# A gated Fourier and expert-mixing kernel: sums of the hidden DFT begun earlier with two raw buffers, gate products stored a piece later, z loaded ahead, row transposes spaced anew

## The chip, the core and the metric

The kernel runs on one core of one Trainium2 chip. The time is device microseconds (us) of one execution. TensorE is called PE, VectorE DVE, ScalarE ACT, GpSimd POOL, and the queue that issues most loads SP. The kernel before was timed three times: 816.06, 817.18 and 818.11 us; the median is 817.18 us. The profile is one further execution of the same program, which took 815.7 us.

## The reference

With x of 2048 rows (the sequence) by 640 columns (hidden), cut to what is computed:

```
a = x @ dft_hid_re.T;  b = x @ dft_hid_im.T
y = dft_seq_re @ a - dft_seq_im @ b               # Fourier part
q = x @ w_q  -> 32 heads, two halves of 128
s1 = q1 @ k1.T;  s2 = q2 @ k2.T                    # 16 scores each
best two of s1, best two of s2, best two of their sums -> expert numbers, softmax g
out = sum over heads and picks of g * gelu(x . u[expert]) * v[expert]    # 256 experts
result = sig * y + (1 - sig) * out,   sig = sigmoid(sum(x * gate_w))
```

Every fp32 product is made of three matmuls (`mm3`, lines 123 to 127): each operand is split into a rounded high part and a low rest, and high-high, high-low and low-high are added up in PSUM.

## The kernel before

**Pieces.** The sequence DFT comes first and runs for most of the span. Two matrices (real, imaginary) by 4 column blocks of 512 give 8 *quarters* q of 16 *pieces* n each, 128 pieces in all. `seq_piece(n)` (line 193) starts the load of piece n+5 on SP, splits piece n+3 (high part on ACT, low part on POOL, `split_piece`, line 160), and multiplies x, kept in SBUF as the tiles X0 to X15, with piece n: 5 banks by 3 matmuls, 15 matmuls of 512 columns. The five products stay in banks 0 to 4 for a quarter. At a quarter's last piece ACT copies them into the five staging slots ST. Then `load_row` (line 180) loads the gate row, `gate_piece` (line 184) multiplies the five slots by it on DVE and issues each one's store to the DRAM scratch P (`pd`) on the ACT queue, right behind its multiply. For the first quarter the row is loaded at piece 18 and multiplied at piece 19; for the later ones the row is loaded at the quarter's last piece and multiplied at the second piece of the next quarter.

**What runs beside the pieces.** `at(n, f)` hangs a function on piece n, and `follow(n)` runs these after the piece's matmuls. A `Pump` (line 41) hands out other work in portions: after every `mm3` it gets a credit of 0.68 us times a share, and takes portions from its queues while it has credit. A function that puts much work on DVE draws credit off. The Pump also has a list `apart` of functions that come a given time after one another (`space`, `tick`): the transposes of the expert rows (`row_tile` in `rows`, line 458) are put there, the first with 12 us (20 us in the last group), the others with 4 us. `tick` adds to `clock` whether the list is empty or not.

In the first quarters the weights of the query are folded with the keys (`w_part`, `w_transposes`, lines 284 and 299), then the scores, the picks on DVE (`topk`, `gates`) and the row transposes follow. After the last row transpose the pool `p3` opens (in the loop, line 865), and `experts(g)` (line 512) begins for two groups of 16 *chunks*: for each chunk DVE builds two one-hot tiles `pt` and `qt` (lines 528 to 530), PE makes 16 small matmuls (line 550) into bank 5 or 6 in turn, in the last part always into bank 7, and DVE sums them into `cd` (lines 535 and 537). One chunk's tiles are built ahead of the matmuls of the one before.

**The last part.** The hidden DFT is made as a block product with sums and differences, 2 halves b by 35 *steps* m. The units of 5 steps each are a11, a12, s1, s2, s4, s3, a22. In the last quarter the sums of the DFT matrix D are made: `load_dt` (line 597) loads two rows of blocks into one raw tile, `make_sums` (line 610) makes five sums on DVE into one tile `tf`, `split_sums` (line 623) splits them on ACT, POOL and DVE into tiles that lie over the parts of x that are no longer needed. `load_v` and `split_v` do the same for v. Each step splits the operand of the step five later (`split_step`, line 684). The operands are loaded from P by SP into raw tiles that `take` hands out, `add_a` adds the ones that are sums. `load_z` loads the gate row, the activations and the expert sums gd for one block of 512 columns, `split_z` multiplies them and splits the result into `zo`, and `z_group` multiplies `zo` with v at the end of a12, of s4 and elsewhere. `load_z` first drains the Pump until the experts of its half are summed. It stands at steps 3 and 21 of each half, `split_z` four steps later.

All engines run their own instructions in program order. A waiting instruction holds up all that stands behind it on its engine or queue.

Of the kernel before, what the change touches and what calls it, by code (L numbers as in the profile page):

```python
# [8 lines left out]
F32 = mybir.dt.float32  # L9
F32R = mybir.dt.float32r  # L10
# [6 lines left out]
P = 128  # L17
S = 2048
D = 640
# [5 lines left out]
NT = S // P  # L25
NP = NT // 2
TC = 512
NC = S // TC
NPC = 2 * NC * NT
KD = D // P  # L30
# [10 lines left out]
class Pump:  # L41
# [8 lines left out]
        self.clock = 0.0  # L50

    def space(self, f, us):
        self.apart.append((f, us))

    def tick(self, us):
# [33 lines left out]
def gated_mix_kernel(ctx: ExitStack, tc: tile.TileContext, xT, xn, dreT, dimT, wsre, wsim, wq, kT, uT, vv, gw, out):  # L89
    nc = tc.nc  # L90
# [3 lines left out]
    big = ctx.enter_context(tc.tile_pool(name="big", bufs=1))  # L94
# [9 lines left out]
    def bank(n, shape=(P, TC), dt=F32):  # L104
        return psum.tile(list(shape), dt, name=f"b{n}", tag=f"b{n}")
# [4 lines left out]
    def ps_t(shape, dt=F32):  # L110
        return bank(7, shape, dt)
# [3 lines left out]
    def stage():  # L115
        return ST[:, rotate("st", 5)]

    def split(f, h, l, eng):

        nc.scalar.activation(h, f, AF.Copy)  # L120
        eng.tensor_sub(l, f, h.bitcast(F32))  # L121

    def mm3(o, wh, wl, ah, al, first, last, more=False):

        nc.tensor.matmul(o, wh, ah, start=first, stop=False, skip_group_check=more)  # L125
        nc.tensor.matmul(o, wh, al, start=False, stop=False, skip_group_check=more)  # L126
        nc.tensor.matmul(o, wl, ah, start=False, stop=last, skip_group_check=more)  # L127

    pd = dram.tile([2, NC, KD, P, TC], F32, name="pd")
# [3 lines left out]
    bg = Pump()  # L133

    def run_bg(us):
        bg.run(us, 0.95 if p3 is None else 0.9 if last_part else 1.0)


    WU = big.tile([P, 2 * KD * (HH * E + NE)], F32R, name="WU", tag="WU")
# [10 lines left out]
    pf, psp, X, xr = {}, {}, {}, {}  # L150

    def load_piece(n):
        if n < NPC:
            w, c, s = pieces[n]
            pf[n] = big.tile([P, TC], F32, name="wf", tag="wf", bufs=5)
            nc.sync.dma_start(pf[n], (wsre, wsim)[w][c, s])
# [3 lines left out]
    def split_piece(n):  # L160
        if n < NPC:
            psp[n] = WS[:, n % 4, 0], WS[:, n % 4, 1]
            split(pf.pop(n), *psp[n], nc.gpsimd)
# [4 lines left out]
    def at(n, f, *args):  # L168
        then.setdefault(n, []).append(lambda: f(*args))

    def follow(n):
        for f in then.pop(n, ()):
            f()


    banks = []
    p3, last_part = None, False
    grow, staged = {}, {}

    def load_row(q):  # L180
# [3 lines left out]
    def gate_piece(q):  # L184
        g = grow.pop(q)
        w, c = divmod(q, NC)
        for d in range(KD):
            f = staged.pop((q, d))
            nc.vector.scalar_tensor_tensor(f, f, -1.0 if w else 1.0, g, op0=OP.mult, op1=OP.mult)
            bg.credit -= 0.75  # L190
            nc.scalar.dma_start(pd[w, c, d], f)

    def seq_piece(n):
        w, c, s = pieces[n]
        if s == 0:
            banks[:] = [bank(d) for d in range(KD)]
        load_piece(n + 5)
        split_piece(n + 3)
        h, l = psp.pop(n)
        for d in range(KD):  # L200
            ds = slice(d * P, (d + 1) * P)
            mm3(banks[d], X[s][:, 0, ds], X[s][:, 1, ds], h, l, s == 0, s == NT - 1)
            if s == NT - 1:
                staged[n // NT, d] = f = stage()
                nc.scalar.activation(f, banks[d], AF.Copy)
            run_bg(0.68)

    for q in range(2 * NC):
        n = NT * (q + 1)
        at(n + (2 if q == 0 else -1), load_row, q)  # L210
        at(n + (3 if q == 0 else 1), gate_piece, q)


    p1_stack = ctx.enter_context(ExitStack())
# [32 lines left out]
    t = ps_t([P, 512])  # L247
# [70 lines left out]
    xf, xs = {}, {}  # L318
# [19 lines left out]
    n = 3  # L338
    for m in range(0, NWQ, 2):
        n = 4 + m if m < 14 else 17 + (m - 14) * 10 // 16  # L340
# [37 lines left out]
    picked, rowed = set(), set()  # L378
# [121 lines left out]
    for p in range(NP):  # L500
        n = N0 + 5 * p
# [4 lines left out]
    N1 = N0 + 5 * NP  # L506
# [88 lines left out]
    TS, T = {}, {}  # L595

    def load_dt(k):
        T["f"] = big.tile([P, 2, D], F32, name="dt", tag="xf")
        for w in range(2):
            nc.sync.dma_start(T["f"][:, w], (dreT, dimT)[w][k])  # L600

    def t_sum(k, n, a):

        if n < 2:
            return TS[k][:, (2 * n + a) * 2 * P:][:, :2 * P]
        if n == 2:
            return TS[5 + k // 2][:, (2 * (k % 2) + a) * 2 * P:][:, :2 * P]
        return DD[:, 0, a, k, 2 * P:4 * P] if n == 3 else TS[k][:, PAIR + a * P:][:, :P]

    def make_sums(k):  # L610
        if k == 0:
            T["t"] = big.tile([P, 9 * P], F32, name="tf", tag="xl")
        f, t = T["f"], T["t"]
        b11, b12, b21, b22 = (f[:, n, a * 2 * P:(a + 1) * 2 * P] for n in range(2) for a in range(2))
        t1, t5, t3, t6 = (t[:, n * 2 * P:(n + 1) * 2 * P] for n in range(4))
        nc.vector.tensor_sub(t[:, :4 * P].rearrange("p (n d) -> p n d", n=2), f[:, :, 0:2 * P], f[:, :, 2 * P:4 * P])
        nc.vector.scalar_tensor_tensor(t3, t1, -1.0, b22, op0=OP.mult, op1=OP.subtract)
        nc.vector.tensor_sub(t5, t1, t5)
        nc.vector.tensor_sub(t6, b22, b12)
        nc.vector.tensor_sub(t[:, 8 * P:], f[:, 1, 4 * P:], f[:, 0, 4 * P:])  # L620
        bg.credit -= 3.0

    def split_sums(k):
        for n in [k] + ([5 + k // 2] if k % 2 == 0 else []):
            TS[n] = big.tile([P, 2 * D], F32R, name="ts", tag=f"X{n}")
        t = T["t"]
        t1, t5, t3, t6 = (t[:, n * 2 * P:(n + 1) * 2 * P] for n in range(4))
        for n, f in enumerate((t1, t3, t5, t6, t[:, 8 * P:])):
            split(f, t_sum(k, n, 0), t_sum(k, n, 1), nc.gpsimd if n < 3 else nc.vector)
        bg.credit -= 1.0  # L630

    def load_v():
# [12 lines left out]
        return TS[5 + a][:, PAIR:].rearrange("p (k d) -> p k d", k=2)  # L645

    for k in range(KD):
        at(NPC - 13 + 2 * k, load_dt, k)
        at(NPC - 11 + 2 * k, make_sums, k)
        at(NPC - 10 + 2 * k, split_sums, k)  # L650
    at(NPC - 2, load_v)
    at(NPC - 1, split_v)


    raw_free, raw_tags = deque(), [("wf", 1)] * 5 + [(f"X{s}", 2) for s in range(10, 16)] + [("xf", 2)]
# [28 lines left out]
    def split_step(m):  # L684
        if m < 2 * NSTEP:
            b, (u, k) = m // NSTEP, divmod(m % NSTEP, KD)
            what = UNITS[u]
            key = (b, "s" if what in ("s1", "s2", "s4") else what, k)
            sp[m] = ring(m)[:, 0], ring(m)[:, 1]
            split(raw[key], *sp[m], nc.vector if what in ("s2", "s3") else nc.gpsimd)  # L690
            bg.credit -= 0.8 if what in ("s2", "s3") else 0.0
            if what in ("a11", "a12", "a22", "s3", "s4"):
                give(key)
# [148 lines left out]
    for b in range(2):  # L842
        M = NPC + b * NSTEP
        for k in range(KD):
            at(M - (8 if b else 6) + k, load_a, b, "a11", k, 1, 1)
            at(M - (4 if b else 2) + k, load_a, b, "a12", k, 1, 2)
            at(M + k, load_a, b, "s", k, 2, 2)
            at(M + k, load_a, b, "s3", k, 2, 1)
            at(M + 4 + k, add_a, b, "s", "s3", k, False)
            at(M + 5 + k, load_a, b, "a11", k, 1, 1)  # L850
            at(M + 8 + k, add_a, b, "s", "a11", k, False)
            at(M + 8 + k, add_a, b, "s3", "a11", k, True)
            at(M + 10 + k, load_a, b, "a12", k, 1, 2)
            at(M + 13 + k, add_a, b, "s", "a12", k, True)
            at(M + 21 + k, load_a, b, "a22", k, 2, 2)
        for n, i in ((0, 3), (1, 21)):
            at(M + i, load_z, b, n)
            at(M + i + 4, split_z, b, n)

    prep_split = {NPC - 4: (0,), NPC - 3: (1,), NPC - 2: (2,), NPC - 1: (3, 4)}  # L860
    WP = None
    for n in range(N0, NPC):
        seq_piece(n)
        follow(n)
        if n >= N1 and p3 is None and len(rowed) == NT and n % NT not in (0, NT - 1):
            p2_stack.close()
            p3 = ctx.enter_context(tc.tile_pool(name="p3", bufs=1, reuse_waits="tile"))
            pools.append(p3)
            WP = p3.tile([P, 2, 2, TC], F32R, name="WP")
            for g in range(2):  # L870
                bg.add(experts(g), late=True)
        for m in prep_split.get(n, ()):
            split_step(m)
    assert p3 is not None

    last_part = True
# [49 lines left out]
```

## Time and profile before

| what | value |
|---|---|
| median of three runs | 817.18 us |
| the profiled execution | 815.7 us |
| its span, first to last instruction | 813.7 us |
| PE busy | 789.6 us (97%) |
| DVE busy | 539.5 us (66%) |
| POOL busy | 340.9 us (42%) |
| ACT busy | 271.8 us (33%) |
| mean granted PE clock | 0.987 |

Matmuls overlap, so PE's busy time says only that some matmul was under way. In the timeline each row has the start, the duration, the engine, the line and the operation with its tiles. A bracket gives the time that the engine stood idle before it and what released it. In the table by stretches each engine's busy time is followed by its number of instructions; the clock is that which the throttle granted to PE (1.00 is full).

### The profile page before, as it was taken

The numbers are of one execution on the slowest core, as the hardware profiler recorded it, in microseconds if no ns is written. First come the engines' busy times: TensorE is split into PE (matmuls) and PEld (weight loads), VectorE is DVE, ScalarE is ACT, GpSimd is POOL, SyncE is SP. The second block draws the span as 40 slices with busy tenths as digits, with TensorE's granted clock in tenths as the row PEclk, the third lists the DMA queues.
The fourth block names the chain that finished last, engine by engine and source line by source line (L and its number), as shares of the span: only waits on it lengthen the run. The fifth ranks groups of instructions, "written<-read, shape, count | busy, mean of one in ns | idle before, by whom it ended". The sixth has DMA issues, their size and how long they took to land.

```text
span 813.7 us, 10931 instructions
## 1 busy us (share of the span) xinstructions
PE 789.6 (97%) x4167; PEld 627.9 (77%) x4167; DVE 539.5 (66%) x652; ACT 271.8 (33%) x444; POOL 340.9 (42%) x239
## 2 busy tenths in 40 slices
PE   8999899999999999999998999999999897999997
PEld 6677567888888888888886777777778675888886
DVE  4851201376887799689878397767768899637651
ACT  3434124322317134322613721311313442434350
POOL 5433133415334142342414674333336664567370
PEclk9999999999999999999999999999999998999999
DMA  9876984603023230214213533234333597397521
GB/s 344 304 280 185 321 317 130 212 1 110 14 98 102 86 110 14 97 48 139 99 41 114 166 120 92 91 117 130 95 119 117 176 294 235 91 296 235 178 94 64
DMA packets 62643, 119.55 MB, mean 147 GB/s; under 512 B 8832, under 2 KB 15616, under 8 KB 62336
## 3 DMA queue, kind: packets, MB, share of 16 engines
q1 hardware_dynamic: 49984, 101.55, 37.6%
q10 hardware_dynamic: 12608, 17.31, 5.9%
q8 instruction: 32, 0.52, 0.3%
q14 instruction: 19, 0.16, 0.1%
HBM read 98.91 MB, written 19.93 MB: 146 GB/s over the span
## 4 chain that ended last, share of the span: by engine, by line
PE 82%; DMA 6%; DVE 6%; ACT 2%; issue 2%; SPq 1%; POOL 1%; ACTq 0%; DVEq 0%; POOLq 0%
PE b L125 26%; PE b L127 25%; PE b L126 25%; PE b L291 2%; DMA ra<-pd 1%; DMA xr<-in_xn 1%; PE b L550 1%; DMA grow<-gdr 1%; DMA wf<-in_wsre 1%; ACT rows L467 1%; PE b L303 1%; DMA wf<-in_wsim 1%; DMA pd<-ST 1%; POOL WS L121 0%; DVE pt L530 0%
## 5 line engine op out<-in xcount | busy, mean ns | idle before, releaser
L121 POOL TENSOR_TENSOR WS<-wf,WS 128x512 fp32r<-128x512 f32 x128 | 186.8, 1465 | 297.1 <-ACT WS L120 295.6
L125 PE MATMUL b<-WS,X 128*128 128x512 f32 x640 | 257.1, 402 | 1.2 <-ACT X L120 1.2
L127 PE MATMUL b<-WS,X 128*128 128x512 f32 x640 | 250.6, 392 | 0.7 <-DVE X L121 0.6
L126 PE MATMUL b<-WS,X 128*128 128x512 f32 x640 | 250.6, 392 | 0.6 <-POOL WS L121 0.6
L125 PEld LDWEIGHTS b<-WS,X 128*128 128x128 f32 x640 | 120.5, 188 | 34.9 <-issue 7.9
L127 PEld LDWEIGHTS b<-WS,X 128*128 128x128 f32 x640 | 120.6, 188 | 27.6 <-DVE X L121 1.5
L126 PEld LDWEIGHTS b<-WS,X 128*128 128x128 f32 x640 | 120.7, 189 | 24.2 <-POOL WS L121 1.0
L120 ACT ACTIVATE WS<-wf 128x512 fp32r<-128x512 f32 x128 | 80.9, 634 | 139.1 <-PE b L127 85.6
L405 DVE TENSOR_REDUCE mm<-sc 128x64 f32<-128x1024 f32 x32 | 39.0, 1219 | 49.8 <-ACT sc L391 49.2
L121 POOL TENSOR_TENSOR xl<-xf,xh 128x640 fp32r<-128x640 f32 x16 | 32.6, 2059 | 73.5 <-ACT xh L120 73.5
L391 ACT ACTIVATE sc<-b 128x512 f32<-128x512 f32 x32 | 20.7, 647 | 127.2 <-PE b L127 114.5
L125 PE MATMUL b<-WU,xh 128*128 128x512 f32 x160 | 62.5, 391 | 0.0
L126 PE MATMUL b<-WU,xh 128*128 128x512 f32 x160 | 62.3, 389 | 0.0
L127 PE MATMUL b<-WU,xl 128*128 128x512 f32 x160 | 62.3, 389 | 0.0
L121 POOL TENSOR_TENSOR WS<-ra,WS 128x512 fp32r<-128x512 f32 x32 | 47.1, 1490 | 30.1 <-ACT WS L120 30.1
L535 DVE TENSOR_TENSOR tmp<-b,mask 128x512 f32<-128x512 f32 x32 | 22.0, 689 | 39.0 <-PE b L550 39.0
L306 DVE TENSOR_TENSOR WU<-b,WU 128x512 fp32r<-128x512 f32 (+1 forms) x16 | 7.8, 490 | 60.0 <-ACT WU L305 60.0
L407 DVE TENSOR_TENSOR eq<-sc,mm 128x1024 f16<-128x1024 f32 x32 | 46.3, 1446 | 1.1
L529 DVE TENSOR_TENSOR qt<-rows,wtab 128x1024 f16<-128x1024 f16 x32 | 32.8, 1025 | 14.3 <-PE b L466 14.3
L411 DVE TENSOR_REDUCE rr<-eq 128x64 f16<-128x1024 f16 x32 | 39.0, 1220 | 1.1
L467 ACT ACTIVATE rows<-b 128x384 f16<-128x384 f16 x16 | 30.7, 1916 | 26.6 <-PE b L466 26.6
L120 ACT ACTIVATE WS<-ra 128x512 fp32r<-128x512 f32 x46 | 28.1, 628 | 33.3 <-PE b L127 10.6
(145 smaller groups left out, 1256.7 us busy)
## 6 DMA issues: line engine op xcount, KB each, us to landing
wq<-in_wq SPq DMA_DIRECT2D x32, 640.0 KB, 6.3
ra<-pd SPq DMA_DIRECT2D x70, 256.0 KB, 4.6
wf<-in_wsre SPq DMA_DIRECT2D x64, 256.0 KB, 5.5
wf<-in_wsim SPq DMA_DIRECT2D x64, 256.0 KB, 2.7
pd<-ST ACTq DMA_DIRECT2D x40, 256.0 KB, 2.3
xr<-in_xn SPq DMA_DIRECT2D x16, 320.0 KB, 6.2
xf<-in_xT SPq DMA_DIRECT2D x16, 320.0 KB, 3.3
out_y<-ST ACTq DMA_DIRECT2D x7, 512.0 KB, 3.4
```

Source lines behind the costliest of these rows:

```text
L120: nc.scalar.activation(h, f, AF.Copy)
L121: eng.tensor_sub(l, f, h.bitcast(F32))
L125: nc.tensor.matmul(o, wh, ah, start=first, stop=False, skip_group_check=more)
L126: nc.tensor.matmul(o, wh, al, start=False, stop=False, skip_group_check=more)
L127: nc.tensor.matmul(o, wl, ah, start=False, stop=last, skip_group_check=more)
L391: nc.scalar.activation(scs[i].rearrange("p h e -> p (h e)")[:, c], ps, AF.Copy)
L405: nc.vector.tensor_reduce(m, sc, op=OP.max, axis=AX.X)
L407: nc.vector.tensor_tensor(eq, sc, m[:, :, None].to_broadcast([P, HH, E]), op=OP.is_equal)
L411: nc.vector.tensor_reduce(r, eq, op=OP.max, axis=AX.X)
L467: nc.scalar.activation(ROWS[i // 8][:, :, :, i % 8], t, AF.Copy)
L529: nc.vector.tensor_tensor(qt, row(1), wt, op=OP.is_equal)
L535: nc.vector.tensor_tensor(tmp, t.rearrange("p m (e t) -> p (m e) t", t=4), mask4[:, None, :].to_broadcast([P, 8 * E, 4]), op=OP.mult)
```

## The change

- `Pump.space` sets `clock` to zero when the list `apart` is empty, so the first transpose of a group really comes 12 or 20 us after it is put there.
- The Pump's share is 0.75 instead of 1.0 in the last 16 pieces (`ending`).
- The gate row is loaded at the last piece but one of a quarter (from the third quarter on), the multiply stands at the first piece of the next quarter, and the five stores stand one piece behind it, in a function of their own. For the first quarter the multiply moves from piece 19 to 23, the stores to 24.
- Loads of the rows of D begin at piece 111 instead of 115, in two raw buffers in turn; sums follow at 114 instead of 117, splits at 115 instead of 118, over other tiles of x; one of three splits on POOL moves to DVE. v is loaded at piece 124 instead of 126 and split at 126 instead of 127.
- The first `load_z` of each half stands at step -1 (the last piece, or step 34) instead of step 3, its `split_z` at step 3 instead of 7.
- `p3` may open at a quarter's first piece, but no longer at its last but one.

```diff
     def space(self, f, us):
+        if not self.apart:
+            self.clock = 0.0
         self.apart.append((f, us))
...
-        bg.run(us, 0.95 if p3 is None else 0.9 if last_part else 1.0)
+        bg.run(us, 0.95 if p3 is None else 0.9 if last_part else 0.75 if ending else 1.0)
...
             bg.credit -= 0.75
-            nc.scalar.dma_start(pd[w, c, d], f)
+            staged[q, d] = f
+
+    def store_piece(q):
+        w, c = divmod(q, NC)
+        for d in range(KD):
+            nc.scalar.dma_start(pd[w, c, d], staged.pop((q, d)))
...
-        at(n + (2 if q == 0 else -1), load_row, q)
-        at(n + (3 if q == 0 else 1), gate_piece, q)
+        at(n + (2 if q == 0 else -2 if q > 1 else -1), load_row, q)
+        at(n + (7 if q == 0 else 0), gate_piece, q)
+        at(n + (8 if q == 0 else 1), store_piece, q)
...
-        T["f"] = big.tile([P, 2, D], F32, name="dt", tag="xf")
+        T[k] = big.tile([P, 2, D], F32, name="dt", tag=("xf", "xh")[k % 2])
...
-            TS[n] = big.tile([P, 2 * D], F32R, name="ts", tag=f"X{n}")
+            TS[n] = big.tile([P, 2 * D], F32R, name="ts", tag=f"X{(1, 3, 4, 5, 6, 0, 2, 7)[n]}")
...
-            split(f, t_sum(k, n, 0), t_sum(k, n, 1), nc.gpsimd if n < 3 else nc.vector)
+            split(f, t_sum(k, n, 0), t_sum(k, n, 1), nc.gpsimd if n < 2 else nc.vector)
...
-        at(NPC - 13 + 2 * k, load_dt, k)
-        at(NPC - 11 + 2 * k, make_sums, k)
-        at(NPC - 10 + 2 * k, split_sums, k)
-    at(NPC - 2, load_v)
-    at(NPC - 1, split_v)
+        at(NPC - 17 + 2 * k, load_dt, k)
+        at(NPC - 14 + 2 * k, make_sums, k)
+        at(NPC - 13 + 2 * k, split_sums, k)
+    at(NPC - 4, load_v)
+    at(NPC - 2, split_v)
...
-        for n, i in ((0, 3), (1, 21)):
+        for n, i in ((0, -1), (1, 21)):
...
     for n in range(N0, NPC):
+        ending = n >= NPC - 16
...
-        if n >= N1 and p3 is None and len(rowed) == NT and n % NT not in (0, NT - 1):
+        if n >= N1 and p3 is None and len(rowed) == NT and n % NT not in (NT - 2, NT - 1):
```

**First place: the ACT queue in the second quarter.** The rows are ACT's instructions around piece 19, with WU the folded weights, wp their raw form, wf the raw pieces and WS their split form. Before:

```order
L305 ACTIVATE WU_73<-b7_756 128x4x128
L120 ACTIVATE WS_76<-wf_701 128x512
L191 DMA pd_69<-ST_68 128x512 x5
L305 ACTIVATE WU_73<-b7_806 128x128
L297 ACTIVATE wp_816<-b5_763 128x320
L297 ACTIVATE wp_816<-b6_770 128x320
```

The same engine in the changed kernel, around piece 24:

```order
L313 ACTIVATE WU_73<-b7_941 128x4x128
L122 ACTIVATE WS_76<-wf_878 128x512
L198 DMA pd_69<-ST_68 128x512 x5
L313 ACTIVATE WU_73<-b7_988 128x128
L305 ACTIVATE wp_998<-b5_948 128x320
L305 ACTIVATE wp_998<-b6_955 128x320
```

The five stores stand between the same neighbours, five pieces later; the multiplies that they wait for stand one piece ahead of them.

**Second place: the SP queue where the last quarter ends.** ra are the raw tiles; loads from gdr, actd and gd are those of z. Before:

```order
L182 DMA grow_5300<-gdr_72 128x512
L673 DMA ra_5249<-pd_69 128x512
L673 DMA ra_5251<-pd_69 128x512 x2
L673 DMA ra_5187<-pd_69 128x512
L673 DMA ra_5308<-pd_69 128x512 x2
L673 DMA ra_5110<-pd_69 128x512
L673 DMA ra_5157<-pd_69 128x512
L673 DMA ra_5216<-pd_69 128x512
L673 DMA ra_5328<-pd_69 128x512 x2
L673 DMA ra_5330<-pd_69 128x512
L701 DMA ra_5330<-gdr_72 128x512
L704 DMA ra_5332<-actd_70 128x512
```

The changed kernel:

```order
L184 DMA grow_5099<-gdr_72 128x512
L681 DMA ra_5055<-pd_69 128x512
L681 DMA ra_5010<-pd_69 128x512
L681 DMA ra_5107<-pd_69 128x512
L709 DMA ra_5109<-gdr_72 128x512
L712 DMA ra_5109<-actd_70 128x512
L715 DMA ra_5036<-gd_71 128x128 x4
L712 DMA ra_5133<-actd_70 128x512
L715 DMA ra_5133<-gd_71 128x128 x4
L681 DMA ra_5135<-pd_69 128x512 x2
```

Before, twelve loads from P stand between the gate row and z; now there are three, and the loads of the s tiles (ra_5135 and on) come behind z.

**Third place: DVE at the end of step 34**, where the first half of the last part ends. pt and qt are the one-hot tiles of a chunk, tmp and cd its sums. Before, the last two chunks are summed in step 24, and these are DVE's rows there and behind them:

```order
L535 TENSOR_TENSOR tmp_5760<-b7_5743,mask4_144 128x512
L537 TENSOR_REDUCE cd_4394<-tmp_5760 128x8x16
L535 TENSOR_TENSOR tmp_5789<-b7_5772,mask4_144 128x512
L537 TENSOR_REDUCE cd_4394<-tmp_5789 128x8x16
L717 TENSOR_SCALAR ra_5110<-ra_5110 128x512
L720 TENSOR_TENSOR ra_5328<-ra_5328,ra_5332 128x512
```

In the changed kernel, the last rows of a run that begins with the sums of chunk 11 of the second group:

```order
L536 TENSOR_TENSOR pt_5883<-rows1_1192,wtab4_142 128x1024
L537 TENSOR_TENSOR qt_5884<-rows1_1192,wtab4_142 128x1024
L538 TENSOR_TENSOR pt_5883<-pt_5883,rows1_1192 128x1024
L543 TENSOR_TENSOR tmp_5905<-b7_5888,mask4_144 128x512
L545 TENSOR_REDUCE cd_4489<-tmp_5905 128x8x16
L536 TENSOR_TENSOR pt_5908<-rows1_1192,wtab4_142 128x1024
L537 TENSOR_TENSOR qt_5909<-rows1_1192,wtab4_142 128x1024
L538 TENSOR_TENSOR pt_5908<-pt_5908,rows1_1192 128x1024
L543 TENSOR_TENSOR tmp_5930<-b7_5913,mask4_144 128x512
L545 TENSOR_REDUCE cd_4489<-tmp_5930 128x8x16
L543 TENSOR_TENSOR tmp_5950<-b7_5933,mask4_144 128x512
L545 TENSOR_REDUCE cd_4489<-tmp_5950 128x8x16
```

On PE the matmuls of the last five chunks (11 to 15) now stand in one run of 80 between the last matmul of step 34 and the first of step 35, all into bank 7; three of the five chunks are built on DVE within that run. The row transposes of the last group stand at pieces 80 to 84 instead of 75 to 78, and the experts begin six pieces later.

More of the change, by code (lines that the diff above doesn't have):

```diff
@@ L176, in gated_mix_kernel @@
     banks = []
-    p3, last_part = None, False
+    p3, last_part, ending = None, False, False
     grow, staged = {}, {}
@@ L597, in load_dt @@
     def load_dt(k):
-        T["f"] = big.tile([P, 2, D], F32, name="dt", tag="xf")
+        T[k] = big.tile([P, 2, D], F32, name="dt", tag=("xf", "xh")[k % 2])
         for w in range(2):
-            nc.sync.dma_start(T["f"][:, w], (dreT, dimT)[w][k])
+            nc.sync.dma_start(T[k][:, w], (dreT, dimT)[w][k])
     def t_sum(k, n, a):
@@ L612, in make_sums @@
             T["t"] = big.tile([P, 9 * P], F32, name="tf", tag="xl")
-        f, t = T["f"], T["t"]
+        f, t = T.pop(k), T["t"]
         b11, b12, b21, b22 = (f[:, n, a * 2 * P:(a + 1) * 2 * P] for n in range(2) for a in range(2))
```

## The prediction

> **What bounds the kernel now.** I read the chain of waits first, then busy times by stretches, then the rows where PE stood idle.
>
> ```profile
> PE 82%; DMA 6%; DVE 6%; ACT 2%; issue 2%; SPq 1%; POOL 1%; ACTq 0%; DVEq 0%; POOLq 0%
> ```
>
> The chain goes through PE for 82% of the span. What another engine adds counts only where PE waits for it, so a change that leaves the matmuls alone is worth the PE time it frees minus the PE time it blocks. Going through the span in stretches of 20 us, I looked for those with a clock below 1.00 in the middle of the work. In each row stand the stretch, its length, then busy time and instructions of PE, weight loads, DVE, ACT and POOL, then the clock, the DMA share and GB/s.
>
> ```profile
> 80.00:100.00 20.00, 17.86 (x110) 11.98 (x108) 3.79 (x6) 2.62 (x5) 3.67 (x3) 1.00 0.93 298
> 100.00:120.00 20.00, 18.84 (x110) 12.59 (x111) 1.97 (x4) 5.87 (x13) 6.42 (x5) 0.91 0.85 313
> 440.00:460.00 20.00, 15.99 (x71) 12.17 (x70) 5.46 (x10) 9.63 (x11) 9.83 (x8) 0.91 0.18 60
> 640.00:660.00 20.00, 16.31 (x88) 12.28 (x87) 18.03 (x21) 9.86 (x19) 12.58 (x11) 0.83 0.67 212
> 660.00:680.00 20.00, 15.28 (x73) 11.65 (x72) 19.16 (x20) 6.32 (x11) 14.97 (x10) 0.86 0.90 285
> ```
>
> There are four such places, and the change touches each. Each costs twice: the idle time, and a stretch at half rate behind it. Where matmul rows are complete I count the second from their starts, else as 0.09 x 20 = 1.8 us for a clock of 0.91.
>
> **The change part by part.**
>
> *Stores of the first quarter.*
>
> ```profile
> 95.54 3.10 DVE L189 SCALAR_TENSOR_TENSOR ST<-ST,grow 128x512 f32<-128x512 f32 x5 [6.15 <-DMA grow<-gdr]
> 96.26 4.10 ACTq L191 DMA_DIRECT2D pd<-ST  x5
> 97.47 0.39 PE L127 MATMUL b<-WS,X 128*128 128x512 f32 x1
> 101.16 1.09 PE L303 MATMUL b<-identf,wp 128*128 128x128 f32 x4 [3.30 <-ACT wp L297]
> ```
>
> DVE waited 6.15 us for the gate row. The five stores, each behind its multiply, held ACT's queue until 100.4, and PE stood 3.30 us for wp. In the changed order the row has five pieces, not one, between load and multiply, and the stores have another piece (15 matmuls spaced 0.23, 3.4 us). Both waits go: 3.30 + 1.8 = **5.1 us**. The multiply now sits at the head of DVE's queue at piece 23, where that engine is 10 to 19% busy (rows 80 and 100); five at 0.62 us are hidden there. The later quarters' stores, a piece behind, can only help ACT. Nothing here is late next.
>
> *Row transposes.*
>
> ```profile
> 440.93 0.23 PE L465 MATMUL b<-ident,rp 128*128 128x128 f16 x1 [0.68 <-DVE rp L444]
> 442.15 0.23 PE L465 MATMUL b<-ident,rp 128*128 128x128 f16 x1 [0.99 <-DVE rp L444]
> 444.72 0.23 PE L466 MATMUL b<-ident,gs 128*128 128x128 f16 x1 [2.34 <-DVE gs L454]
> ```
>
> PE waited 4.01 us for DVE's picks; with the clock 0.91, **5.8 us**. The last transposes move from pieces 75-78 to 80-84, some 17 us later, seven times the longest wait; I take all of it. The price: the experts begin six pieces (20 us) later and finish less before the last part, which matters below.
>
> *Sums of D.* WP and DD are operands of the last part's step 0.
>
> ```profile
> 643.85 0.39 PE L126 MATMUL b<-WP,DD 128*128 128x512 f32 x1
> 644.07 0.39 PE L127 MATMUL b<-WP,DD 128*128 128x512 f32 x1
> 648.15 0.79 PE L125 MATMUL b<-WP,DD 128*128 128x512 f32 x1 [3.69 <-DVE tmp L535]
> ...
> 652.58 0.63 PE L126 MATMUL b<-WP,DD 128*128 128x512 f32 x1
> 653.01 0.63 PE L127 MATMUL b<-WP,DD 128*128 128x512 f32 x1
> ```
>
> Step 0's second product waits for a bank that DVE clears (tmp) only behind the last sums. Starts 644.07 to 648.15 instead of 0.23: 3.85 us. The eleven spacings to 653.01 take 4.86 instead of 2.5: 2.4 us. Together **6.2 us**. With sums four pieces (14 us) sooner, DVE is through with them before step 0, and I take all of it. Two things use up slack: the split that goes from POOL to DVE, five times over 16 pieces, and the gate multiply of the last quarter but one.
>
> *z ahead of the s tiles.*
>
> ```profile
> 671.51 0.39 PE L127 MATMUL b<-WS,DD 128*128 128x512 f32 x1
> 675.62 0.80 PE L125 MATMUL b<-zo,vxh 128*128 128x512 f32 x1 [3.72 <-ACT zo L120]
> 677.42 0.79 PE L126 MATMUL b<-zo,vxh 128*128 128x512 f32 x1 [1.00 <-POOL zo L121]
> ...
> 681.00 0.43 PE L125 MATMUL b<-zo,vxh 128*128 128x512 f32 x1
> ```
>
> z_group waited 675.62 - 671.51 - 0.23 = 3.88 us, then 1.80 - 0.23 = 1.57, then eight spacings of 0.45 (3.58 us) where 1.84 would do, 1.7 more: **7.2 us**. DVE's part of z came late:
>
> ```profile
> 672.10 1.48 DVE L717 TENSOR_SCALAR ra<-ra 128x512 f32<-128x512 f32 x1
> ...
> 675.54 0.69 DVE L721 TENSOR_TENSOR ra<-ra 128x512 f32<-128x512 f32 x1
> L121 POOL TENSOR_TENSOR WS<-ra,WS 128x512 fp32r<-128x512 f32 x32 | 47.1, 1490 | 30.1 <-ACT WS L120 30.1
> ```
>
> These 4.1 us of z now stand at step 3, four steps (4 x 9 x 0.23 = 8.3 us) sooner, and the wait of 3.72 goes. In exchange the two splits of zo on POOL, 1.49 each, stand ahead of the split that step 9 needs, which I find 1 us late: **+1 us**. Ends: 0, if POOL's idle time takes them up; 6, if DVE, busy 18.03 and 19.16 of 20 us in 640:680, is no sooner with the a12 tiles.
>
> *load_z of the second half, at step 34.* This is new, and no row of before shows it. load_z first drains the Pump. At step 3 of the second half nothing is left; now five chunks of the second group are, and they run back to back between steps 34 and 35. All use bank 7, so each chunk's 16 matmuls wait until DVE has read the one before, and three must be built by DVE in between. One chunk without disturbance:
>
> ```profile
> 601.08 0.69 DVE L535 TENSOR_TENSOR tmp<-b,mask 128x512 f32<-128x512 f32 x1 [3.22 <-PE b L550]
> 601.80 0.69 DVE L537 TENSOR_REDUCE cd<-tmp 128x128 f32<-128x512 f32 x1
> 602.40 0.95 DVE L528 TENSOR_TENSOR pt<-rows,wtab 128x1024 f16<-128x1024 f16 x1
> 603.28 0.68 DVE L529 TENSOR_TENSOR qt<-rows,wtab 128x1024 f16<-128x1024 f16 x1
> 603.88 0.68 DVE L530 TENSOR_TENSOR pt<-pt,rows 128x1024 f16<-128x1024 f16 x1
> ```
>
> From start to start tmp takes 0.72 and cd 0.60, the build to its end 2.16: 3.48 us a chunk. The second chunk, built ahead, starts 1.2 us after the first (0.41 of matmuls, 0.8 for tmp), the other three 3.48 apart, so the last ends at 1.2 + 3 x 3.48 + 0.4 = 12.05. Five chunks alone are 5 x 0.41 = 2.05, which PE would spend anyway. Loss: 10.0 us. The same build beside POOL's work took
>
> ```profile
> 622.05 1.22 DVE L528 TENSOR_TENSOR pt<-rows,wtab 128x1024 f16<-128x1024 f16 x1
> 623.20 1.22 DVE L529 TENSOR_TENSOR qt<-rows,wtab 128x1024 f16<-128x1024 f16 x1
> 624.34 1.78 DVE L530 TENSOR_TENSOR pt<-pt,rows 128x1024 f16<-128x1024 f16 x1
> ```
>
> 4.07 us, 1.91 more. Three such builds make the other end, 10.0 + 5.7 = 15.7. POOL has about two splits outstanding when the drain begins, one build's worth, and stands idle after; I take 11. This overlap has a rule: the Trainium skill (SBUF — State Buffer, "Who interferes with whom") says that a DVE operation with two SBUF inputs and a GpSimd operation that reads SBUF exclude each other for a whole instruction; 4.07 against 2.16 agrees. By it, the split moved to DVE would stretch too.
>
> Then the clock. In the drain PE works about 0.4 us in every 3.5. At the other places idle times of 3.7 cost 2.4 and 1.7 us afterwards, and PE also comes out at half rate here: 2.4 (0 if it does not drop; 2.9 if six steps' worth of spacings are slow). Total for the drain: **13.4 us**. The Trainium skill (TensorE: Matmul & The Clock Gate, "HAM oscillation — how this bites in real kernels") warns only of idle gaps above 3.4 us; the gaps here are about 3.1, so by it the sum would be 2.4 lower. The row of 440:460 differs: its longest gap was 2.34 and the clock was still 0.91.
>
> Behind the drain the expert sums go out and come back:
>
> ```profile
> gd<-cd SPq DMA_DIRECT2D x4, 512.0 KB, 5.0
> 655.45 6.87 DVE L189 SCALAR_TENSOR_TENSOR ST<-ST,grow 128x512 f32<-128x512 f32 x5
> ```
>
> The write takes 5.0 us, and SP holds the loads of z and then one of a12 behind it. About 1 us of slack remains by the steps' lengths: 0, at worst 3. The last multiply (second row, 6.87 us) moves a piece ahead, and so leaves DVE freer in step 2.
>
> **Sum** against the profiled execution (815.7; its span is 813.7 and 2.0 lie around it): -5.1 - 5.8 - 6.2 - 7.2 = -24.3; +13.4 + 1.0 = +14.4; 815.7 - 9.9 = 805.8. The median of the runs, 817.18, is 1.5 above that execution, so I forecast **807** us.
>
> **The rivals.**
>
> *The drain is cheap.* If the clock holds and POOL does not interfere: 10.0 instead of 13.4, and no +1: 807.3 - 4.4 = 803. For it: the drain's gaps are short. Against: the 0.91 in 440:460.
>
> *z late again.* DVE is nearly full in 640:680, so z at step 3 may be no sooner done than it was: 7.2 comes back less the 1.0, 807.3 + 6.2 = 813.5. The other end of the contended builds plus a late a12 (4.7 + 3) would give 815.
>
> *It does not do what it says.* Were the wait of the stores or of the transposes to stay, because the gate row or the picks slip as far as their users: 5.1 or 5.8 back, 812.4 to 813.1. Against: 17 us of room each, where the waits were 2 to 6.
>
> *Slower.* DVE is behind by more than it can catch up when step 0 comes. The sums, a gate multiply, the moved split and a later expert all stand in the last 14 pieces; ACT's eviction of bank 0 stands behind splits that wait for DVE. Once DVE's backlog at piece 126 is over about 2 us (the margin at step 0, from 0.6 us for ACT plus two chunks' sums at 0.7 each), both the old wait at step 0 (6.2) and that of z (7.2) return on top of the drain: 807.3 + 13.4 = 820.7. Against: the sums stand 14 us sooner, and the Pump hands out less in the last 16 pieces.
>
> **How the numbers follow.** Forecast as summed (803.5 to 811): 0.58. Cheap drain (801 to 803.5): 0.09. z late or the drain contended (811 to 814.7): 0.15. A part without effect (about 812.5): 0.05. Such losses together, within 0.3% of 817.18 (814.7 to 819.6; this is about what a measurement of this kernel can tell from no change): 0.07. Both waits return: 0.06. Faster: 0.58 + 0.09 + 0.15 + 0.05 = 0.87. The range is 801 to 814: it takes in both ends of the drain (-3.4, +4.7) and the return of one wait.
>
> **What would show it.** In the changed profile: no PE idle time released by wp near 97 us, nor by rp or gs near 440, and a clock of 1.00 in those stretches; step 0 and the first z_group without an idle time over 0.5 us. New, between 690 and 730 us: four idle times of PE, one below 1 us and three near 3, released by DVE's tmp or pt, and a clock near 0.85 in that stretch. The forecast is wrong if no such group appears (the five chunks were done sooner), or if the first z_group waits again.

## The result and the profile after

| | before | after |
|---|---|---|
| median of 4 runs each | 816.62 us | 809.87 us |
| lowest and highest | 815.75, 818.11 | 809.80, 810.21 |
| the profiled execution, and its span | 815.7, 813.7 us | 809.91, 808.1 us |

A fourth run of the kernel before makes its median 816.62 instead of 817.18. The ratio after to before is 0.9916, with a 95% interval of 0.9899 to 0.9933: faster by 0.8%. The forecast was 807 us with a range of 801 to 814. The sum against the profiled execution was 805.8 us, which came out at 809.91: of the 9.9 us that the sum promised, a little over half came.

First the chain of waits of the changed kernel, by engine:

```profile
PE 85%; DMA 6%; issue 4%; POOL 2%; DVE 1%; SPq 1%; ACT 0%; DVEq 0%; POOLq 0%; ACTq 0%
```

PE's share rose from 82 to 85% and DVE's fell from 6 to 1%: the places where PE waited for DVE are mostly gone. Then the table by stretches (columns as above):

```profile
80.00:100.00 20.00, 20.00 (x132) 13.38 (x131) 1.67 (x3) 5.64 (x11) 4.13 (x4) 1.00 0.95 313
100.00:120.00 20.00, 20.00 (x121) 14.05 (x120) 5.80 (x9) 5.29 (x12) 5.94 (x5) 1.00 0.90 329
420.00:440.00 20.00, 20.00 (x90) 16.55 (x89) 19.52 (x26) 7.28 (x13) 13.71 (x9) 1.00 0.44 146
440.00:460.00 20.00, 20.00 (x94) 16.22 (x93) 9.57 (x9) 11.48 (x18) 14.82 (x11) 1.00 0.65 222
620.00:640.00 20.00, 20.00 (x117) 16.07 (x116) 16.46 (x19) 6.59 (x13) 7.68 (x5) 1.00 0.69 210
640.00:660.00 20.00, 16.16 (x75) 11.86 (x74) 14.97 (x15) 7.32 (x13) 14.46 (x10) 0.91 0.82 283
700.00:720.00 20.00, 13.36 (x126) 10.67 (x118) 18.54 (x24) 3.54 (x6) 8.77 (x6) 0.91 0.10 40
720.00:740.00 20.00, 16.62 (x89) 13.76 (x90) 9.47 (x16) 2.52 (x4) 4.45 (x4) 0.75 0.57 166
```

The stretches near 100 and 440 us are full and at clock 1.00, and so is the one with step 0 (626.8 us now). Two places are left: 640 to 660, and 700 to 740, which is new. In the second, the timeline of PE from the last matmul of step 34 on:

```profile
711.52 0.39 PE L129 MATMUL b<-WS,ts 128*128 128x512 f32 x1
711.84 0.44 PE L558 MATMUL b<-qt,pt 128*64 128x64 f16 x16
714.65 0.44 PE L558 MATMUL b<-qt,pt 128*64 128x64 f16 x16 [2.37 <-DVE tmp L543]
717.78 0.64 PE L558 MATMUL b<-qt,pt 128*64 128x64 f16 x16 [2.68 <-DVE tmp L543]
720.90 0.64 PE L558 MATMUL b<-qt,pt 128*64 128x64 f16 x16 [2.48 <-DVE tmp L543]
724.02 0.64 PE L558 MATMUL b<-qt,pt 128*64 128x64 f16 x16 [2.48 <-DVE tmp L543]
724.59 0.80 PE L127 MATMUL b<-WS,DD 128*128 128x512 f32 x1
...
729.88 0.47 PE L127 MATMUL b<-WP,DD 128*128 128x512 f32 x1
```

This is the drain: five chunks one behind the other, four idle times, each ended by DVE's tmp. A spacing is the time from one matmul's start to the next one's, 0.23 us at full clock. A chunk between other matmuls takes 0.60 us of PE: 0.46 until the next matmul starts (699.44 to 700.13 less one spacing) and 0.14 in the seven spacings behind it, which are a little longer than 0.23 (to 701.86). From 711.52 to 724.59 are 13.07; less 0.23 and five times 0.60, **9.9 us** are lost. The twelve spacings to 729.88 take 5.29 instead of 2.72: **2.6 us** of slow clock. Together the drain costs 12.5 us.

The other place, PE's rows in steps 6 to 9 of the first half:

```profile
642.88 0.50 PE L128 MATMUL b<-WP,DD 128*128 128x512 f32 x1 [0.81 <-POOL WP L123]
...
645.86 0.50 PE L127 MATMUL b<-WS,DD 128*128 128x512 f32 x1 [0.49 <-ACT WS L122]
647.21 0.50 PE L128 MATMUL b<-WS,DD 128*128 128x512 f32 x1 [0.84 <-POOL WS L123]
...
651.38 0.69 PE L128 MATMUL b<-WS,DD 128*128 128x512 f32 x1 [1.68 <-POOL WS L123]
...
754.75 0.50 PE L127 MATMUL b<-WS,DD 128*128 128x512 f32 x1 [1.47 <-ACT ST L835]
```

Adding up what the spacings from 641.68, the matmul before the first wait, to 654.86 have beyond the usual 0.23 and one chunk, with the slow ones behind 651.38, gives **6.5 us**. (The expectations of the runs below put this place at 5.9 us.) The last row is a single wait in the second half, **1.8 us** by its spacings. The first z_group itself waits for nothing.

The ledger, each term from the spacings of the same matmuls in both timelines (gains positive; a chunk between other matmuls counts 0.60):

| term | forecast | measured |
|---|---|---|
| wait for wp (first quarter's stores) | 5.1 | 4.95 |
| last row transposes | 5.8 | 6.1 |
| three earlier transposes, 0.36 each | 0 | 1.1 |
| step 0 (sums of D) | 6.2 | 6.5 |
| first z_group | 7.2 | 7.3 |
| new waits in steps 6 to 9 | -1.0 | -6.5 |
| drain at step 34 | -13.4 | -12.5 |
| behind the drain | 0 | -1.8 |
| sum | 9.9 | 5.15 |

With the 0.42 us by which the first pieces happened to start sooner this is 5.57, as the last matmul has it: it stands at 809.19 before and at 803.62 after.

### The profile page after: what moved, and what is told of

It reads as the page before. It is cut to its first block, busy times and chain, and to the rows that moved or that the text cites. A ratio compares the mean times of both kernels' runs of the same rounds, so it can differ in the third digit from the quotient of the medians.

```text
span 808.1 us, 10931 instructions
## 1 busy us (share of the span) xinstructions
PE 786.0 (97%) x4167; PEld 627.4 (78%) x4167; DVE 540.1 (67%) x657; ACT 274.7 (34%) x444; POOL 341.1 (42%) x234
## 4 chain that ended last, share of the span: by engine, by line
PE 85%; DMA 6%; issue 4%; POOL 2%; DVE 1%; SPq 1%; ACT 0%; DVEq 0%; POOLq 0%; ACTq 0%
PE b L127 28%; PE b L129 27%; PE b L128 27%; PE b L299 2%; DMA ra<-pd 2%; POOL WS L123 2%; DMA xr<-in_xn 1%; PE b L558 1%; DMA ra<-actd 1%; DMA wf<-in_wsre 1%; DMA pd<-ST 1%; PE b L311 1%; POOL zo L123 0%; DVE ST L191 0%; POOL WP L123 0%
## 5 line engine op out<-in xcount | busy, mean ns | idle before, releaser
L123 POOL TENSOR_TENSOR WS<-wf,WS 128x512 fp32r<-128x512 f32 x128 | 189.4, 1484 | 283.5 <-ACT WS L122 281.3
L123 POOL TENSOR_TENSOR WS<-ra,WS 128x512 fp32r<-128x512 f32 x32 | 48.8, 1549 | 42.9 <-ACT WS L122 35.8
L191 DVE SCALAR_TENSOR_TENSOR ST<-ST,grow 128x512 f32<-128x512 f32 x40 | 37.4, 995 | 18.7 <-ACT DD L122 10.3
L415 DVE TENSOR_TENSOR eq<-sc,mm 128x1024 f16<-128x1024 f32 x32 | 43.8, 1369 | 1.1
L123 POOL TENSOR_TENSOR WP<-ra,WP 128x512 fp32r<-128x512 f32 x18 | 29.0, 1619 | 28.6 <-ACT WP L122 28.5
L684 DVE TENSOR_TENSOR ra<-ra 128x512 f32<-128x512 f32 x40 | 35.2, 919 | 8.1 <-DMA ra<-pd 6.5
```

Source lines behind the costliest of these rows:

```text
L415: nc.vector.tensor_tensor(eq, sc, m[:, :, None].to_broadcast([P, HH, E]), op=OP.is_equal)
L684: nc.vector.tensor_add(raw[b, o, k], raw[b, o, k], raw[b, what, k])
```

## The experiments

The kernel before ran again beside the experiments and its medians were between 816.83 and 818.48 us, so each experiment's ratio to it is given as well as its time. The changed kernel has 0.9916. What a run loses at a place is added up from the spacings of its matmuls, as above, in its one profiled execution.

### Do the gains belong to the parts they were put down to?

**The stores alone**, on the kernel before:

```
-        at(n + (3 if q == 0 else 1), gate_piece, q)
+        at(n + (7 if q == 0 else 1), gate_piece, q)
+        at(n + (8 if q == 0 else 1), store_piece, q)
```

> The kernel before with the first quarter's multiply at piece 23 and its stores at 24, all else as before. Theory: the wait for wp near 97 us and the slow clock behind it go, 5.0 us, and nothing else moves: 811.5 to 813 us where the kernel before has 816.6 to 818. Rival (the stores hold up something else five pieces later): 814 us or more.

811.41 us, ratio 0.9931 (0.9903 to 0.9958). The wait for wp is gone and the other three stand as they were (3.75 at step 0, 3.73 and 1.00 at z_group). The forecast of 5 us lies within the interval; the time is 0.1 below the band.

**The spacing of the transposes alone**: in `space`, `if not self.apart: self.clock = 0.0`, on the kernel before.

> The kernel before with the two lines in space alone (the clock starts when the list was empty). Theory: the waits for rp and gs near 440 us go (6.0 us), and three small ones for earlier transposes (1.1 us); two chunks instead of none are left for the drain behind step 35, 1.2 to 2 us; the other waits of before stay: 810.5 to 812 us. Rival (the later experts put more on DVE in the last part, so that the waits at step 0 and at z_group grow): 813 to 817 us.

813.37 us, ratio 0.9946 (0.9927 to 0.9966), in the band of the rival. The waits for rp and gs are gone, as in the theory, but a new one stands in the second half, in the timeline of PE:

```profile
750.38 0.50 PE L127 MATMUL b<-zo,vxh 128*128 128x512 f32 x1 [2.64 <-ACT zo L122]
751.75 0.80 PE L128 MATMUL b<-zo,vxh 128*128 128x512 f32 x1 [0.86 <-POOL zo L123]
```

By the spacings it costs 6.7 us with its slow clock. Later experts put the drain between step 35 and z (two chunks, at 727.44 and 728.71), the write of gd and the loads of z follow, and z is late. So the spacing pays at one place and charges at another; the charge falls where load_z stands.

**The sums alone**, on the kernel before (two raw buffers, 111, 114 and 115 instead of 115, 117 and 118, v at 124 and 126, other tiles, one split to DVE):

> The kernel before with the sums of D alone moved (two raw buffers, load at piece 111, sums 114, splits 115, v at 124 and 126, other tiles, one split from POOL to DVE). Theory (two separate waits): the wait at step 0 goes, 6.5 us, and the z_group wait of 7.2 us stays: 810 to 812 us. Rival 1 (z was late only because DVE was behind): both go, 803 to 806 us. Rival 2 (the bank is held by a chunk at piece 127 anyway): 815 us or more.

810.84 us, ratio 0.9916 (0.9889 to 0.9944). PE's rows at z_group:

```profile
670.59 0.49 PE L125 MATMUL b<-zo,vxh 128*128 128x512 f32 x1 [1.22 <-ACT zo L120]
672.73 0.79 PE L126 MATMUL b<-zo,vxh 128*128 128x512 f32 x1 [1.65 <-POOL zo L121]
```

No wait is left at step 0, and z_group still loses 6.2 of 7.3 us by its spacings. The two waits are separate but for the 1.1 us; z is late for its own place in the order.

### The drain

**The share back at 1.0 in the last 16 pieces**, on the changed kernel: two chunks are left for step 34 instead of five.

```
-        bg.run(us, 0.95 if p3 is None else 0.9 if last_part else 0.75 if ending else 1.0)
+        bg.run(us, 0.95 if p3 is None else 0.9 if last_part else 1.0 if ending else 1.0)
```

> The changed kernel with the share of the last 16 pieces back at 1.0. By program order two chunks instead of five are left for step 34 (the others go to pieces 116 to 126), and neither has to be built in the drain. Theory (each drained chunk that DVE must build costs PE 3.1 us): three times 3.1 = 9.4 us less, and up to 2.5 less where the clock does not drop: 798 to 801 us. Rival (the smaller share is what keeps DVE from being late at step 0): the wait at step 0, 6.5 us in the kernel before, comes back in part or whole: 803 to 808 us, with an idle time of PE before step 0's second product.

801.83 us, ratio 0.9812 (0.9786 to 0.9838): 8.0 us less than the changed kernel. The drain is now

```profile
715.77 0.44 PE L558 MATMUL b<-qt,pt 128*64 128x64 f16 x16 [2.37 <-DVE tmp L543]
716.14 0.50 PE L127 MATMUL b<-WS,DD 128*128 128x512 f32 x1
```

The second chunk starts 2.81 us behind the first (712.96). From the last matmul of step 34 (712.64) to 716.14 are 3.50 us; less 0.23 and twice 0.60, 2.1 are lost, and 1.7 of slow clock follow: 3.8 instead of 12.5. Step 0 does not wait, so the rival falls: the smaller share bought nothing there and cost three chunks in the drain. The time is 0.8 above the band, because the second chunk costs 2.1 us although it is built ahead, and the clock still drops.

### The waits of steps 6 to 9

**z back behind the s tiles** in the first half, on the changed kernel:

```
-        for n, i in ((0, -1), (1, 21)):
+        for n, i in ((0, -1 if b else 3), (1, 21)):
```

> The changed kernel with the first half's load_z and split_z back at steps 3 and 7; the second half keeps them at step 34 and 38. Theory A (the waits of steps 2 to 9 come from z standing ahead): these 5.9 us go and the wait of 7.2 us before the first z_group comes back: 811 us. Theory B (they come from the late multiply): the first two, 0.8 and 1.3 us, stay, and z_group waits besides: 813 to 815 us. A third possibility (with the sums of D sooner DVE is free, and z would be in time at step 7 as well): no z_group wait, 805 to 809 us.

812.32 us, ratio 0.9937 (0.9916 to 0.9957).

```profile
653.77 0.79 PE L127 MATMUL b<-zo,vxh 128*128 128x512 f32 x1 [4.51 <-ACT zo L122]
655.57 0.80 PE L128 MATMUL b<-zo,vxh 128*128 128x512 f32 x1 [1.00 <-POOL zo L123]
```

All waits of steps 6 to 9 are gone, and z_group loses 7.9 us. Theory A holds: z ahead exchanges 7.9 us for 6.5. The last multiply and its stores stand as late here as in the changed kernel (634.03; the last store leaves at 640.60), so by themselves they do not make the waits. The question is then what in the new order makes the 6.5. In the changed kernel's timeline (rows of SP, DVE, ACT's queue, ACT and POOL picked out):

```profile
628.31 1.75 SPq L715 DMA_DIRECT2D ra<-gd  x4
632.53 30.12 SPq L681 DMA_DIRECT2D ra<-pd  x24
...
633.42 5.28 DVE L191 SCALAR_TENSOR_TENSOR ST<-ST,grow 128x512 f32<-128x512 f32 x5
...
635.23 5.05 ACTq L198 DMA_DIRECT2D pd<-ST  x5
640.41 0.63 ACT L122 ACTIVATE WP<-ra 128x512 fp32r<-128x512 f32 x1 [8.97 <-DVE ra L729]
645.18 0.63 ACT L122 ACTIVATE WS<-ra 128x512 fp32r<-128x512 f32 x1 [4.14 <-DMA ra<-pd]
...
647.12 2.98 POOL L123 TENSOR_TENSOR zo<-ra,zo 128x512 fp32r<-128x512 f32 x2
650.06 4.19 POOL L123 TENSOR_TENSOR WS<-ra,WS 128x512 fp32r<-128x512 f32 x3
```

Three suspects: the five stores hold ACT's queue until 640.28, and the WP split starts 0.13 us later, whatever the profile names as its releaser; the a12 tiles are loaded behind z's eleven loads (the gate row, two of actd, eight of gd), so the WS split at 645.18 waits for its tile; and POOL splits zo ahead of the WS that PE then misses.

**The last multiply and its stores a piece sooner** (quarter 7 at pieces 127 and 128 instead of 128 and 129):

> The changed kernel with the last quarter's gate multiply one piece sooner (piece 127, ahead of a chunk's build on DVE) and its stores one piece sooner (step 0). Theory B (the 5.9 us that PE loses in steps 2 to 9 start with this multiply: it is late on DVE, the stores behind it hold ACT's queue for 5 us, and the s tiles can be loaded only after the stores): these waits shrink to under 1.5 us, 805 to 806 us. Rival A (the two zo splits of z stand ahead of a WS split on POOL, whatever the multiply does): 1.7 us of idle time and the slow clock behind it, together 3.9 us, stay: 807.5 to 809 us.

809.10 us, ratio 0.9902 (0.9876 to 0.9929), not to be told from the changed kernel. Of 6.5 us, 5.0 stay, with

```profile
649.98 0.50 PE L128 MATMUL b<-WS,DD 128*128 128x512 f32 x1 [1.81 <-POOL WS L123]
```

The wait for WP is gone and that for WS is not.

**The a12 tiles ahead of z in SP's queue**:

```
-            at(M - (4 if b else 2) + k, load_a, b, "a12", k, 1, 2)
+            at(M - 4 + k if b else M - 2 + min(k, 1), load_a, b, "a12", k, 1, 2)
```

> The changed kernel with the first half's a12 tiles 1 to 4 all loaded at the last piece, ahead of z in SP's queue (they stood at the last piece and steps 0 to 2, tiles 2 to 4 behind z's ten loads and between the loads of the s tiles). Theory C (the 5.9 us lost in steps 6 to 10 come from the a12 tiles landing late, so that ACT and POOL split them late): these waits go, 804 to 806 us, without an idle time over 0.5 us before the first z_group. Rival A (POOL's order, zo ahead of the WS splits): the idle time of 1.7 us and its slow clock stay, 807.5 to 810 us.

809.45 us, ratio 0.9904 (0.9872 to 0.9937). Of 6.5 us, 5.3 stay, at another tile, and 0.6 appear a unit later:

```profile
645.59 0.50 PE L127 MATMUL b<-WP,DD 128*128 128x512 f32 x1 [2.37 <-ACT WP L122]
```

Now WS is in time and WP is late: ACT's split of it starts only at 644.91, 0.13 us after the last store has left.

**split_z one step later** in the first half (step 4 instead of 3):

> The changed kernel with the first split_z at step 4 instead of 3, so that one more WS split stands ahead of the two zo splits on POOL. Rival A: the idle time of 1.7 us before step 9 shrinks by a split or more, and the slow stretch behind it goes: 805 to 807 us. Theory C (the tiles land late, whatever POOL's order is): the waits stay within 1.5 us, 808.5 to 811 us.

811.84 us, ratio 0.9938 (0.9919 to 0.9957), a little above both bands: 5.8 us stay and 0.8 appear a unit later, so POOL's order is not the cause (rival A falls). C alone is not the cause either, by the run before.

**Both single edits together**:

> The changed kernel with both single edits together: the last quarter's multiply and stores a piece sooner, and the first half's a12 tiles all loaded ahead of z. Each alone left 4.8 and 5.2 of the 5.9 us. Theory D (two waits stand one behind the other: ACT's queue held by the stores behind the late multiply, and a12 tiles landing late behind z; removing one uncovers the other): together under 1.5 us is left, 804 to 806 us. Rival (the DMA engines, 0.85 to 0.90 busy there, are what is short, in whatever order): the wait moves once more and 4 us or more stay, 807.5 to 810 us.

807.25 us, ratio 0.9879 (0.9858 to 0.9901), between the two bands. 1.1 us are left in steps 6 to 9 (one idle time of 0.81), and 1.5 appear a unit later:

```profile
656.75 0.50 PE L127 MATMUL b<-WS,DD 128*128 128x512 f32 x1 [1.19 <-ACT ST L835]
```

In this trace it is as theory D says: two waits stood one behind the other, and either edit alone only uncovered the other. The last store leaves at 636.38 (640.28 in the changed kernel), and ACT splits the a12 tile of step 8 at 637.55 (645.18). The rival falls: the DMA engines were fuller than in the changed kernel (0.98 and 1.02 in 630:640 and 640:650, against 0.85 and 0.90), and only 2.6 us of waits are left. The gain is 3.9 us by the spacings and 2.6 by the medians, less than the 4 to 6 expected; the intervals of this run and of the two single edits overlap, so that the two edits work only together is read from the traces alone.

### A version without either cost

**No drain**: share 1.0 both in the last 16 pieces and in the last part, and the a12 tiles of both halves ahead of z (`M - 5 + k if b else M - 2 + min(k, 1)`). **All**: the same with the last multiply and stores a piece sooner.

> The changed kernel with the share 1.0 in the last 16 pieces and in the last part, and the a12 tiles of both halves ahead of z. By program order the last chunk comes at step 32, so nothing is drained at step 34. Theory: the drain's 13.3 us go whole (11.6 of them went with two chunks left), and so do the two waits of the second half (1.2 and 1.4 us in that run): 796 to 799 us, with the waits of steps 5 to 9 about as large as before (4 to 5 us). Rival (DVE, asked for more in the last part, is late for the adds and z): 800 to 804 us.

> As the run without a drain, with the last quarter's multiply and stores a piece sooner as well. Theory D: the waits of steps 5 to 9 go too, 792 to 795 us. Rival: they stay, 796 to 799 us.

798.74 us, ratio 0.9769 (0.9752 to 0.9786), and 798.90 us, ratio 0.9773 (0.9756 to 0.9790). No row of PE waits for tmp any more: the drain's cost is gone whole. The waits of steps 5 to 10 remain in both, 5.5 us in the first and 5.4 in the second by the spacings, and a further 1.2 us stands near 679 us in both. The largest row of the first is

```profile
651.73 0.75 PE L128 MATMUL b<-WS,DD 128*128 128x512 f32 x1 [2.40 <-POOL WS L123]
```

so what the two edits brought with the smaller share they did not bring here, and theory D's forecast for the second run (792 to 795 us) missed. Waits of 1.9 and 1.8 us in the second half also stay.

**Chunks later**: as all, with the share 0.6 in steps 0 to 10 and 1.3 after.

> As the run with all edits, but the Pump's share in the last part is 0.6 in steps 0 to 10 and 1.3 after, so that one chunk instead of three stands in steps 2 to 9 and the last still comes before step 34 (step 31). Theory (three chunks between the adds and z on DVE are what kept 5.4 us of waits in steps 5 to 9, where the kernel with the smaller share before step 0 had 1.2 and 1.4): 795 to 797 us. Rival (the loads decide, not DVE): 798 to 800 us.

799.42 us, ratio 0.9791 (0.9766 to 0.9815). 4.7 of 5.4 us stay, and the chunks pushed back make new waits of 3.1 us near 700, among them

```profile
695.88 0.47 PE L127 MATMUL b<-zo,vxh 128*128 128x512 f32 x1 [1.40 <-ACT zo L122]
```

The theory that DVE's chunks in steps 2 to 9 cause them falls in the main. What keeps these 4 to 5 us in the faster kernels stays open. One difference is on record. In the run with both single edits the last multiply started at 627.91 and its last store left 9.1 us behind step 0's first matmul. In the run with all edits a chunk's build stands ahead of the multiply on DVE, and the stores hold ACT's queue longer:

```profile
631.34 6.40 DVE L191 SCALAR_TENSOR_TENSOR ST<-ST,grow 128x512 f32<-128x512 f32 x5
640.79 1.16 ACT L122 ACTIVATE WP<-ra 128x512 fp32r<-128x512 f32 x2 [7.33 <-DMA pd<-ST]
```

There the last store left 11.6 us behind step 0's first matmul, and 12.1 in the run with chunks later. No run took that away, so it is not shown to be the cause.

## Why the prediction came out as it did

- **The four old waits** are worth what the rows said: 24.3 forecast, 24.9 measured, and 1.1 more from three small transposes that the sum left out. Each part, made alone or taken back alone, moved its own wait: the stores that for wp, the spacing those for rp and gs, the sums that at step 0, z ahead that of z_group.
- **The drain** was the main new cost and came where and as described: four idle times, all released by tmp. 13.4 forecast, 12.5 measured; the cycle is 3.12 us instead of 3.48 (pt took 0.68 without POOL, not 0.95), but the second chunk came after 2.81 instead of 1.2, because DVE was still in a build that POOL's splits had stretched (708.98 to 714.00). The two errors nearly cancel. The idle times forecast "one below 1 us and three near 3" were 2.4 to 2.7. Runs with two and with no chunks left behave accordingly.
- **The term that was mis-sized** is "+1 us" for z ahead of the s tiles: it measured 6.5, just beyond the high end (6) that was kept. Two steps failed here. The sum priced z ahead by POOL's two zo splits alone; moving them back left 5.8 us. It left out SP's queue, where z's eleven loads now stand ahead of a12 tiles, which landed late; with z behind again these waits were gone. The other step is "the last multiply moves a piece ahead, and so leaves DVE freer in step 2": it moved ahead in program order, but stood at 633.42, 6.6 us behind step 0's first matmul, behind a stretched chunk build, took 5.28 us, and the stores behind it held ACT's queue. Taking away either one left 5 us or more, and both together 1.1, with the smaller share; with the larger share the same two edits left 5.4, and why stays open.
- **Behind the drain** the forecast was 0 with 3 at worst; 1.8 came, an eviction of bank 0 on ACT (L835, 754.12) behind a split that waits 3.52 us for DVE's adds, the first of which waited 1.12 for a load from P.
- **The rivals.** "z late again" was not what came, though its price was nearly right: z was in time, and its neighbours were late instead. "Slower" fell: step 0 did not wait, and not even with the share at 1.0 did DVE get late there. The cheap drain fell too: the clock dropped. "It does not do what it says" fell: the waits of the stores and of the transposes both went.
- The range held the time, but the mechanism accounts for that only in part: the sum was 4.1 us too low. The 1.5 us added for the median did not apply, and brought the forecast nearer by luck: the changed kernel's runs lie within 0.4 us of its profiled execution, while those of before spread over 2.4 us.

## What to carry to other kernels

When a function that first finishes background work is moved ahead, count what is then left of that work: at the new place it runs alone, at the pace of its slowest engine, and it may cost more than the wait that the move removes. When a load is moved ahead in a queue, what now stands behind it can be late next, and removing one of two waits in a row can merely uncover the second; try the edits together before one of them is dropped. A throttle on background work that was meant to relieve one place should be tested by itself.

## What the runs showed of the hardware

- A DVE operation that meets a POOL split is much longer. These are DVE rows of the changed kernel, first beside POOL's splits where the drain begins, then in the drain with POOL idle:

```profile
710.56 1.77 DVE L537 TENSOR_TENSOR qt<-rows,wtab 128x1024 f16<-128x1024 f16 x1
712.25 1.75 DVE L538 TENSOR_TENSOR pt<-pt,rows 128x1024 f16<-128x1024 f16 x1
...
715.84 0.68 DVE L537 TENSOR_TENSOR qt<-rows,wtab 128x1024 f16<-128x1024 f16 x1
716.44 0.68 DVE L538 TENSOR_TENSOR pt<-pt,rows 128x1024 f16<-128x1024 f16 x1
```

  The first two lie beside POOL's splits of 710.04 to 715.13; behind these POOL is idle until 729.59. The Trainium skill (SBUF — State Buffer, "Who interferes with whom") says that such a pair shares a port exclusively; 1.77 against 0.68 agrees.
- Short idle times can halve the clock, but not always. One of 2.37 with the drain's last chunk was followed by spacings of 0.43 instead of 0.23 (716.95 to 719.92 in the run with two chunks left), while in the run with all edits one of 2.35 us was not, and its granted clock was 1.00 throughout. In steps 6 to 9 of the changed kernel even one of 1.68 us, with 0.49 and 0.84 in the 6 us before it, was followed by seven spacings of 0.43 (651.87 to 654.86). The Trainium skill (TensorE: Matmul & The Clock Gate, "HAM oscillation — how this bites in real kernels") puts the limit at gaps above 3.4 us; here no idle time in the drain was above 2.7, and the clock of 720:740 was 0.75.
- A store can hold its queue after its data is ready. In the run with the a12 tiles first, the multiplies end at 640.08 and the last store goes out at 644.46; the profile names the landing of another store as what ACT waited for:

```profile
644.91 0.63 ACT L122 ACTIVATE WP<-ra 128x512 fp32r<-128x512 f32 x1 [12.09 <-DMA pd<-ST]
```
